# A planned one-core attention kernel: a new table of shifts for its planner, and one more pack of scores for VectorE

## The chip, the cores and the metric

The kernel runs on one core of a Trainium2 chip. The metric is the time of one execution on the device in microseconds. Five engines work side by side: TensorE (PE, with its weight loads as PEld), ScalarE (ACT), VectorE (DVE), GpSimd (POOL), and SyncE (SP), which here only issues DMAs.

## The reference

Two attention blocks read the same input x (2048 tokens of 512, bf16), and a gate mixes their outputs. Block A is softmax attention with 32 heads of 16; block B is linear attention whose features are softmaxes of a learned projection of q and k.

```python
def _A_ref(x, wqkv, wo):
    # q, k, v: 32 heads of 16
    scores = jnp.einsum("bhqd,bhkd->bhqk", q, k) * (Dh ** -0.5)
    p = _softmax(scores, axis=-1)
    o = jnp.einsum("bhqk,bhkd->bhqd", p, v)
    return (lambda x, *d: x.transpose(*d))(o, 0, 2, 1, 3).reshape(B, S, D) @ wo

def _B_ref(x, wqkv, w_phi, wo):
    pq = jnp.einsum("bhsd,hdf->bhsf", q, w_phi)
    pk = jnp.einsum("bhsd,hdf->bhsf", k, w_phi)
    phi_q = jnp.concatenate([_softmax(pq, axis=-1), _softmax(-pq, axis=-1)], axis=-1)
    phi_k = jnp.concatenate([_softmax(pk, axis=-1), _softmax(-pk, axis=-1)], axis=-1)
    kv = jnp.einsum("bhsf,bhsd->bhfd", phi_k, v)
    z  = jnp.einsum("bhsf->bhf", phi_k)
    num = jnp.einsum("bhqf,bhfd->bhqd", phi_q, kv)
    den = jnp.einsum("bhqf,bhf->bhq", phi_q, z)[..., None] + 1e-6
    o = num / den
    return (lambda x, *d: x.transpose(*d))(o, 0, 2, 1, 3).reshape(B, S, D) @ wo

x = A_x
g = _sigmoid((x * gate_w).sum(-1, keepdims=True))
return g * a + (1 - g) * b
```

## The kernel before

**Units and packs.** Block A's scores are cut into units: 128 keys by 512 queries of one head. Four units, four heads of one key tile, make a pack, and there are 512 packs (4 query chunks, 8 groups of heads, 16 key tiles), so 2048 units. A group of scores is written by TensorE (`_scores`, L1013: the contraction over 16 features, zero-padded to 32 rows, takes one of four row strips of the array, so that up to four units share one pass) into a ring of five PSUM banks. ScalarE's exp (L1061, called "exp k" below) reads three units and two units in turn, 1536 or 1024 elements a partition, and writes them to `ET`. The scores of exp k wait for exp k-2, which frees their banks. TensorE then multiplies the exps of a pack with the values (`_values`, L1128, four matmuls of 32 columns, one in each column strip) and adds them up in one PSUM bank for the 16 key tiles of a group.

**Packs for VectorE.** For some packs the exponential isn't made by ScalarE. `AWAY` holds, for each of the 32 groups, five bits: which of the key tiles 1, 4, 7, 10 and 13 go to VectorE. There, `_vector_bits` (L932) turns each unit's scores with one multiply and add into the bits of a bf16 number, which is a rough power of two (`va`), and `_vector_terms` adds two shifted copies of it (`vp`): one by VectorE (L954, for two packs at once 4096 elements wide, for one alone 2048), and one by GpSimd (L969, in two halves a pack). TensorE sums the three terms through the value matmuls (L1128, with `V`, or with `vc`, the scaled values). The units that are left over for ScalarE are grouped three and two in their own order.

**The rest of the work** fills the engines around this: projections of q, k and v (L654 and L727, four matmuls a bank, with a VectorE copy out of PSUM), the product of block B's weights with its feature projection (L1226 transposes them, L1244 multiplies; both need the weights `WB` from DRAM), block B's softmaxes in quads of token tiles (VectorE's tree of maxima L1290, the subtraction L1299, ScalarE's exp L1301 over 2048 elements, twice a quad, then sums and a reciprocal), its sums kv (L1347) and quotients (L1405, L1411, L1413), and the outputs (`_b_out` L1431 and `_out` L1477, copied out by L1490, at the end by L1472, L1483 and L1487). A group's attention is normalized by VectorE (L1149 transposes it out of PSUM, then L1156, L1158, L1160) and turned by DMAs on SP's queue, of the last two groups by VectorE again (L1165). Nine matmuls on a constant tile warm TensorE up at the start (L641).

**The planner.** Nothing of the order is written by hand. Each instruction is an `Op` with an engine, a cost that the author has set, its dependencies, a priority and an earliest pack, and `Plan.order` places them one by one: of the instructions that are ready it takes the one with the lowest priority number. The resulting order of each engine is fixed at build time, and each engine runs its queue strictly in that order, waiting on semaphores. Two lists steer it:

```python
def order(self):
    for o in self.ops:

        d = self.shift.get(o.tag, 0)
        o.prio += d
        o.rel += d if o.rel > -90 else 0
```

`SHIFT` names tags (`b103` is the bits of pack 103, `p10` the value matmuls of pack 10, `k`, `q`, `v` projections, `e`, `h` and others block B's parts, `g` a group's normalization, `y` the outputs) and a number that moves the tag's instructions to earlier or later, in packs.

**Use of the array.** The planner keeps a running sum of how much of the array the matmuls of the last 3 us used, with a score or a value matmul counting a quarter. Where it is low, it adds idle matmuls whose result is zero or is overwritten: `_fill` (L1135, four at a time, in an open accumulation) and whole matmuls ahead of a group of scores (L1034).

```python
low = lambda share: sum(r[1] for r in recent) < share * self.SPAN
while o.filler > o.filled and low(self.SHARE) or (
        o.pad and self.open is None and o.filled < self.PADS and low(self.PAD)):
    o.filled += 1
    recent.append((t, self.FILL))
```

Of the kernel before, what the change touches and what calls it, by code (L numbers as in the profile page):

```python
# [388 lines left out]
class _Kernel:  # L389
# [348 lines left out]
    def _gate(self):  # L738
# [44 lines left out]
    AWAY = (19, 27, 21, 30, 11, 27, 28, 30, 31, 31, 15, 15, 21, 23, 31, 27, 27, 31, 29, 29, 29, 31, 13, 15, 31, 15, 28, 21, 15, 31, 22, 31)  # L783

    SHIFT = (
# [103 lines left out]
    def _plan_vector(self):  # L889
# [3 lines left out]
        pairs = []  # L893
        for g, bits in enumerate(self.AWAY):
            packs = [self.NT * g + self.KT0 + self.KTS * n for n in range(self.NKT) if bits >> n & 1]
# [642 lines left out]
```

## Time and profile before

| | before |
|---|---|
| median of 3 runs | 750.57 us (744.85, 750.57, 750.6) |
| profiled execution, its own time | 745.28 us |
| its span, first to last instruction | 743.5 us |
| ACT busy | 728.4 us (98%) |
| PE busy | 707.1 us (95%) |
| DVE busy | 692.0 us (93%) |
| POOL busy | 277.3 us (37%) |
| mean granted TensorE clock | 0.999 |

The busy time of an engine is the union of its instructions' times. The mean duration of a group can be longer than the pace at which its instructions follow each other, since an engine starts the next before the last has left it; where a number depends on that, the pace is taken from a stretch without idle time. A row of groups reads: line, engine, operation, tiles, shapes and count; then busy time and mean ns of one; then the idle time just before them and what ended it. A row of the chain or the timeline reads: start and length in us, then what ran, and in brackets the idle time before it.

### The profile page before, as it was taken

To read this page: it belongs to the slowest core of one execution; us is meant where nothing else is said; L and a number is where in the kernel's file an instruction comes from. 1 tells how busy PE (TensorE), PEld (TensorE's weight loads), DVE (VectorE), ACT (ScalarE), POOL (GpSimd) and SP (SyncE) were. 2 spreads that over 40 slices of the span, in tenths; PEclk is the share of its full clock that TensorE was granted. 3 is DMA by queue.
4 is the path that set the end of the run, shared out by engine and by line. 5 is a ranking of instruction groups with operands and counts; after the bars stand their busy time and mean duration, and the time that the engine had idled before them with its cause. 6 is when DMAs were issued, how large, how long until landed. Compare 5 with 4: busy or idle time off the path is not lost.

```text
span 743.5 us, 17213 instructions
## 1 busy us (share of the span) xinstructions
PE 707.1 (95%) x7255; PEld 226.9 (31%) x7320; DVE 692.0 (93%) x1093; ACT 728.4 (98%) x636; POOL 277.3 (37%) x275
## 2 busy tenths in 40 slices
PE   8999999999899999999998999999999999999997
PEld 4334234342232222322322233222232223322332
DVE  6898989999998999999999999989999989999994
ACT  5999999999999999999999999999999999999996
POOL 6521331513335534233252442244432253235431
PEclk9999999999999999999999999999999999999999
DMA  9300100101000000000000411220111032104110
GB/s 203 138 9 4 20 4 10 15 2 15 8 12 12 5 17 5 12 11 8 8 10 11 69 16 30 56 48 13 16 37 30 19 67 23 30 20 82 23 23 29
DMA packets 90030, 21.80 MB, mean 29 GB/s; under 512 B 82912, under 2 KB 89440, under 8 KB 89952
## 3 DMA queue, kind: packets, MB, share of 16 engines
q1 hardware_dynamic: 88224, 20.17, 14.1%
q8 instruction: 57, 0.93, 0.6%
q10 hardware_dynamic: 1728, 0.52, 0.3%
q14 instruction: 21, 0.17, 0.1%
HBM read 4.21 MB, written 2.10 MB: 8 GB/s over the span
## 4 chain that ended last, share of the span: by engine, by line
ACT 89%; PE 7%; SPq 2%; DMA 1%; DVE 1%; issue 0%
ACT ET L1061 85%; ACT bq L1301 4%; PE ps L1013 2%; PE ps L1128 2%; PE ps L654 1%; SPq L1383 1%; DMA WB<-in_B_wqkv_dram 1%; PE ps L1431 0%; PE ps L1477 0%; SPq L527 0%; PE ps L727 0%; SPq L542 0%; DVE va L932 0%; ACT xT L1487 0%; DVE VB L1259 0%
## 5 line engine op out<-in xcount | busy, mean ns | idle before, releaser
L1061 ACT ACTIVATE ET<-ps 128x1536 bf16<-128x1536 f32 x616 | 700.9, 1363 | 6.2 <-PE ps L1013 6.0
L969 POOL TENSOR_SCALAR vp<-va 128x1024 uint16<-128x1024 uint16 x258 | 269.5, 1044 | 454.5 <-DVE va L932 120.7
L932 DVE TENSOR_SCALAR va<-ps 128x512 uint16<-128x512 f32 x508 | 332.2, 682 | 22.4 <-PE ps L1013 19.6
L1013 PE MATMUL ps<-qT,kT 32*128 32x512 bf16 x2048 | 310.2, 384 | 15.2 <-ACT ET L1061 8.4
L1013 PEld LDWEIGHTS ps<-qT,kT 32*128 32x128 bf16 x2048 | 81.3, 91 | 265.7 <-ACT ET L1061 160.2
L954 DVE TENSOR_SCALAR vp<-va 128x4096 uint16<-128x4096 uint16 (+1 forms) x143 | 157.7, 1109 | 1.2 <-PE ps L1128 0.8
L1128 PE MATMUL ps<-ET,V 128*32 128x512 bf16 x1540 | 146.1, 385 | 0.2 <-DVE va L932 0.2
L1128 PE MATMUL ps<-vp,vc 128*32 128x512 bf16 x1016 | 91.0, 384 | 1.4 <-DVE vp L954 1.4
L1135 PE MATMUL ps<-kT,zero 128*32 128x512 bf16 x628 | 56.1, 385 | 0.0
L1128 PEld LDWEIGHTS ps<-ET,V 128*32 128x32 bf16 x1540 | 38.0, 95 | 58.7 <-issue 46.8
L654 PE MATMUL ps<-WB,xT 128*128 128x512 bf16 x166 | 50.0, 383 | 4.9 <-issue 2.7
L1128 PE MATMUL ps<-va,V 128*32 128x512 bf16 x508 | 49.8, 385 | 0.0
L1128 PE MATMUL ps<-vp,V 128*32 128x512 bf16 x508 | 46.8, 384 | 1.5 <-DVE vp L954 1.2
L1128 PEld LDWEIGHTS ps<-vp,vc 128*32 128x32 bf16 x1016 | 23.8, 95 | 35.8 <-issue 21.8
L654 PE MATMUL ps<-xT,WA 128*128 128x512 bf16 (+1 forms) x104 | 30.3, 373 | 4.3 <-issue 3.1
L1301 ACT ACTIVATE bq<-bq 128x2048 bf16<-128x2048 bf16 x16 | 32.5, 2035 | 0.0
L1149 DVE STREAM_TRANSPOSE T<-ps 128x512 f32<-128x512 f32 x32 | 22.7, 708 | 5.9 <-PE ps L1128 5.8
L1272 DVE CAST bq<-ps 128x512 bf16<-128x512 f32 x32 | 21.9, 685 | 3.4 <-PE ps L654 3.1
L1135 PEld LDWEIGHTS ps<-kT,zero 128*32 128x32 bf16 x628 | 14.2, 94 | 23.2 <-issue 20.8
L727 PE MATMUL ps<-WA,xT 128*128 128x128 bf16 x256 | 20.5, 220 | 0.2 <-DVE WB L1249 0.2
L1299 DVE TENSOR_TENSOR bq<-bq,btree 128x2048 bf16<-128x2048 bf16 x16 | 20.0, 1248 | 0.1
L654 PEld LDWEIGHTS ps<-WB,xT 128*128 128x128 bf16 x192 | 12.0, 97 | 24.2 <-issue 13.5
(84 smaller groups left out, 343.3 us busy)
## 6 DMA issues: line engine op xcount, KB each, us to landing
turned<-T SPq DMA_DIRECT2D x240, 8.0 KB, 1.8
qT<-qs SPq DMA_DIRECT2D x120, 16.0 KB, 1.8
WB<-in_B_wqkv_dram SPq DMA_DIRECT2D x1, 1536.0 KB, 7.8
out_dram<-WB SPq DMA_DIRECT2D x12, 128.0 KB, 1.7
WA<-in_A_wqkv_dram SPq DMA_DIRECT2D x3, 384.0 KB, 4.6
WoA<-in_A_wo_dram SPq DMA_DIRECT2D x1, 512.0 KB, 8.8
WoB<-in_B_wo_dram SPq DMA_DIRECT2D x1, 512.0 KB, 9.5
WA<-in_A_wqkv_dram ACTq DMA_DIRECT2D x3, 128.0 KB, 4.3
```

Of the source, the lines that this page charges most:

```text
L654: ins = e.matmul(self._bank(job)[:, 0:n], lhs(c), rhs(c), start=(c == 0), stop=(c == 3))
L727: ins = e.matmul(self._bank(job)[:, P * tt:P * tt + P], self.xT[:, c, QCH * j + TOK * tt:QCH * j + TOK * tt + TOK], self.WA[:, 2, c, P * c ...
L932: parts.append(op("DVE", lambda e, j=j, job=job: e.tensor_scalar(self.va[:, pair, side, j, :], self._bank(job), SCALE * LOG2E * 128.0, (12 ...
L954: self.plan.op("DVE", lambda e, k=k, shift=shift: e.tensor_scalar(flat(self.vp[:, k]), flat(self.va[:, pair]), float(shift), None, op0=ALU ...
L969: o = self.plan.op("POOL", lambda e, flat=flat: e.tensor_scalar(flat[0], flat[1], 1.0, float(shift), op0=ALU.mult, op1=ALU.add), 0.08 + n ...
L1013: return e.matmul(out, self.kT[32 * i:32 * i + 32, cp, kt * TOK:(kt + 1) * TOK], self.qT[32 * i:32 * i + 32, s, :], start=True, stop=True, ...
L1061: o = plan.op("ACT", lambda e: e.activation(self.ET[:, a % NS:a % NS + n, :], self.ps[:, self._ring(a):self._ring(a) + n, :], ACT.Exp, sca ...
L1128: ins = e.matmul(self._bank(ot)[32 * i:32 * i + 32, :], V[:, v0:v0 + 32], tile(), start=(kt == 0), stop=(kt == self.NT - 1), tile_position ...
L1135: ins = e.matmul(self._bank(ot)[32 * i:32 * i + 32, :], self.zero[:], self.kT[:, 0, 0:QCH], start=False, stop=False, tile_position=(0, 32 ...
L1149: op("DVE", lambda e: e.transpose(T1[:, side].rearrange("p b s -> p (b s)"), src()), 0.635, deps=last, writes=[b_T1[side]], name="n_t1", p ...
L1272: [lambda e, b, k=k: e.tensor_copy(bq[:, k].rearrange("p (g s v) -> p g s v", g=8, s=2)[:, :, 0, :], b.rearrange("p (g v) -> p g v", g=8))],
L1301: op("ACT", lambda e, side=side: e.activation(sides[side], sides[side], ACT.Exp, scale=1.0 - 2 * side), self.c_act(2048) + 0.04, reads=[bu ...
```

## The change

Only the two tables differ. `AWAY` has 128 bits set instead of 127 and places them otherwise; `SHIFT` has 759 entries instead of 753, nearly all of them new. No function, constant or cost is changed. The author's words for it: the order of work was searched anew, with a charge (in the search, which isn't part of the kernel) for stretches in which TensorE's array is little used; 128 packs for VectorE.

```diff
-    AWAY = (19, 27, 21, 30, 11, 27, 28, 30, 31, 31, 15, 15, 21, 23, 31, 27, 27, 31, 29, 29, 29, 31, 13, 15, 31, 15, 28, 21, 15, 31, 22, 31)
+    AWAY = (23, 26, 30, 22, 27, 26, 21, 27, 31, 15, 31, 30, 19, 15, 22, 30, 31, 31, 15, 31, 28, 31, 30, 30, 30, 31, 21, 15, 29, 15, 30, 31)
 
     SHIFT = (
-        ("a0", -0.5), ("b1", -5.5), ("b103", -11), ("b106", -3.5), ("b109", -11.5), ("b116", -0.5), ("b122", -13),
...
-        ("x81", -2.5), ("x84", 11.5), ("x90", 7.5), ("x93", -14), ("y128", -10.5), ("y256", -0.5), ("y512", -14)
+        ("a0", 1.5), ("a12", -3.5), ("a4", 0.5), ("a8", -6), ("b1", -1), ("b103", 1), ("b113", -4), ("b116", 2.5),
...
+        ("y128", 8), ("y512", -3)
     )
```

Since every engine's order follows from these numbers, nearly every instruction stands elsewhere. Counted in the two built programs, the kinds and numbers of instructions differ in this alone:

| engine, line | before | after |
|---|---|---|
| ACT L1061, 1536 / 1024 / 512 elements | 308 / 308 / 0 | 307 / 307 / 1 |
| DVE L932 | 508 | 512 |
| DVE L954, 4096 / 2048 elements | 109 / 34 | 111 / 32 |
| POOL L969 | 258 | 260 |
| PE L1128, from ET / from va and vp | 1540 / 2032 | 1536 / 2048 |
| PE L1135, fills | 628 | 604 |
| PE L1034, whole matmuls ahead of scores | 15 | 24 |

198 rows, old and new, of the table SHIFT are left out of this document.

## The prediction

> **What bounds the kernel now.** I read the page's first part and its chain, then what ACT waits for, then ACT's groups by form, then the few places where ACT idles, in time.
>
> ```profile
> PE 707.1 (95%) x7255; PEld 226.9 (31%) x7320; DVE 692.0 (93%) x1093; ACT 728.4 (98%) x636; POOL 277.3 (37%) x275
> ACT 89%; PE 7%; SPq 2%; DMA 1%; DVE 1%; issue 0%
> ACT ET L1061 <- PE ps L1013: 6.0, 3, 5.4
> ACT xT L1487 <- PE ps L1477: 3.6, 1, 3.6
> ACT L1061 <- issue: 2.3, 1, 2.3
> ACT ET L1061 <- PE ps L1128: 0.2, 1, 0.2
> ```
>
> PE, DVE and ACT all look full, but only ACT is full by necessity. Its waits (the last four lines: total, times, longest) are 5.4 us for the first scores, 3.6 us at the very end, 2.3 us before the table load, and about 0.8 us in the middle. In between the exps of L1061 run end to end for some 726 us; any work of PE, DVE, POOL or SP that lands in time costs nothing. So the time is: start to first exp, plus ACT's own work, plus ACT's idle time, plus the tail. The question for each edit is which of the four it touches.
>
> ```profile
> L1061 ACT ACTIVATE ET<-ps 128x1536 bf16<-128x1536 f32 x308 | 484.3, 1573 | 6.2 <-PE ps L1013 6.0 <-PE ps L1128 0.2
> L1061 ACT ACTIVATE ET<-ps 128x1024 bf16<-128x1024 f32 x308 | 355.2, 1153 | 0.0
> L1301 ACT ACTIVATE bq<-bq 128x2048 bf16<-128x2048 bf16 x16 | 32.5, 2035 | 0.0
> 120.51 67.85 ACT ET L1061 x60
> 273.48 1.79 ACT bq L1301
> ```
>
> The mean durations overlap (484.3 + 355.2 is more than the 700.9 us of the page's group), so I price exps by the chain's stretch: 60 in 67.85 us are 30 pairs of 2.262 us, five score units a pair. The forms differ by 1573 - 1153 = 420 ns for 512 elements, so a 1536 costs 1.34 us of the row, a 1024 0.92 us, and a 512 (no row) about 0.92 - 0.42 = 0.50 us.
>
> **The change, part by part.** *128 packs instead of 127.* Counted in the two orders, ACT has 308 + 308 exps before and 307 + 307 plus one of 512 after: 2.262 - 0.50 = **1.76 us less**. Bounds: 2.26 if the short exp were free, 2.262 - 0.92 = 1.34 if it cost as much as a 1024. I take 1.76, by the difference of the forms.
>
> ```profile
> L932 DVE TENSOR_SCALAR va<-ps 128x512 uint16<-128x512 f32 x508 | 332.2, 682 | 22.4 <-PE ps L1013 19.6
> L954 DVE TENSOR_SCALAR vp<-va 128x4096 uint16<-128x4096 uint16 x109 | 134.1, 1236 | 0.5 <-PE ps L1128 0.2
> L954 DVE TENSOR_SCALAR vp<-va 128x2048 uint16<-128x2048 uint16 x34 | 23.7, 700 | 0.6 <-PE ps L1128 0.6
> L969 POOL TENSOR_SCALAR vp<-va 128x1024 uint16<-128x1024 uint16 x258 | 269.5, 1044 | 454.5 <-DVE va L932 120.7
> L1135 PE MATMUL ps<-kT,zero 128*32 128x512 bf16 x628 | 56.1, 385 | 0.0
> L1034 PE MATMUL ps<-kT 128*128 128x512 bf16 x9 | 3.4, 383 | 0.4 <-issue 0.3
> ```
>
> The pack goes to DVE: 4 more L932 (4 x 0.682 = 2.7 us), two more wide L954 and two fewer narrow ones (2 x 1.236 - 2 x 0.700 = 1.1 us), 3.8 us in all; POOL gets 2 more L969 (2.1 us). PE gets 4 fewer matmuls of ET, 16 more of va and vp (net +12, four to a pass); the fills of L1135 go from 628 to 604 and the pads of L1034 from 15 (the row holds the records of 9) to 24. A pass or a full matmul paces at 0.22 us (below), so +0.7 - 1.3 + 2.0 = +1.4 us. None is on ACT's path: DVE ends at about 696 of 742 us, PE at 708, POOL at 279. Without that cover DVE's 3.8 us would be the whole price.
>
> *The new order at the start.* Before, PE meets L1226 after its 14th group of scores, and L1226 needs the weights WB.
>
> ```profile
> 16.48 7.75 DMA WB<-in_B_wqkv_dram
> 24.28 0.62 PE L1226 MATMUL ps<-iden,WB 128*128 128x128 bf16 x8 [0.45 <-DMA WB<-in_B_wqkv_dram]
> 25.27 3.84 ACT L1061 ACTIVATE ET<-ps 128x1536 bf16<-128x1536 f32 x3 [0.34 <-PE ps L1013]
> 102.83 2.37 ACT L1061 ACTIVATE ET<-ps 128x1536 bf16<-128x1536 f32 x2 [0.15 <-PE ps L1128]
> 105.53 1.45 ACT L1061 ACTIVATE ET<-ps 128x1536 bf16<-128x1536 f32 x1 [0.33 <-PE ps L1013]
> 70.40 0.54 PE ps L654 x2
> 96.51 0.97 PE ps L654 x4
> ```
>
> WB lands at 24.23; PE stood still 0.45 us, the scores behind L1226 came late, ACT idled 0.34 us. After, the first L1226 stands behind 28 groups, some 14 pairs x 2.262 = 32 us after the first exp: WB has then been there for 16 us. **0.34 us back.** SP's queue up to WB, WoA and WoB is the same, so nothing of the loads is later. The other loads that PE meets early keep slack: x512, landed by 9.9 us, is met after 2 groups instead of 3, at about 10.2 us.
>
> At 102 to 106 us PE itself was short: 4.00 us busy of 4.00, and ACT idled 0.15 + 0.33. Between the 50th and the 100th exp the order has 56 matmuls of L654 and 96 of L727 before, 52 and 80 after. L654 paces at (0.97 - 0.54) / 2 = 0.215 us, a 128-wide L727 at a quarter: 4 x 0.215 + 16 x 0.054 = 1.7 us less for PE there. **0.48 us back** (0 at the least, if the shortage moves).
>
> *The new order at the pairs of L1301.* Scores for exp k wait for exp k-2, so in an L1301 PE runs dry unless other work stands there. The new order puts two L1301 back to back or one exp apart at the 82nd, 473rd and 549th exp, with 4.1, 3.3 and 4.5 us of array work beside them. The tightest is the 549th.
>
> ```profile
> L1490 DVE CAST WB<-ps 128x512 bf16<-128x512 f32 x12 | 8.2, 685 | 0.0
> L1290 DVE TENSOR_TENSOR btree<-btree 128x128 bf16<-128x128 bf16 x16 | 3.5, 218 | 0.0
> L1156 DVE TENSOR_TENSOR rinv<-T,gh 128x32 f32<-128x32 f32 x15 | 2.9, 193 | 0.0
> L1299 DVE TENSOR_TENSOR bq<-bq,btree 128x2048 bf16<-128x2048 bf16 x16 | 20.0, 1248 | 0.1
> ```
>
> From the start of the exp before the first L1301, ACT wants the second after 1.34 + 1.79 + 0.92 = 4.05 us. DVE must by then have done L1490, L1290, L1156, L932 and L1299: 0.685 + 0.218 + 0.193 + 0.682 + 1.248 = 3.0 us, and L1490 waits for an output matmul about 1.0 us in. That is 4.0 us: on the edge, where every L1301 before started without a wait. Bounds 0 and 0.6 us (one DVE copy out of place); I take **0.1 us**, since the durations overlap by some 10%.
>
> *The tail.*
>
> ```profile
> 735.92 0.40 PE L1128 MATMUL ps<-ET,V 128*32 128x512 bf16 x4
> 736.38 0.72 DVE L1149 STREAM_TRANSPOSE T<-ps 128x512 f32<-128x512 f32 x1 [4.41 <-PE ps L1128]
> 25.22 0.55 PE ps L1128 x8
> 26.09 0.33 PE ps L1128 x4
> ```
>
> Before, the last L1149 follows the last four matmuls of ET. After, four of vp stand behind those and L1149 waits for them too: 0.55 - 0.33 = **0.22 us more**. What follows is the same chain. The SP queue is reordered (transfers of qs, T, phiT, nb, out), but counted along both orders the waits on them by PE and DVE keep 0.9 us or more.
>
> Sum on the profiled execution: 745.28 - 1.76 - 0.34 - 0.48 + 0.1 + 0.22 = **743.0**. The page's execution is 0.4 us above the lowest of the runs shown, 744.85, from which the same terms give 742.6. I forecast **742.8**. With the bounds: 744.85 - 2.26 - 0.82 = 741.8 and 745.28 - 1.34 - 0.34 + 0.6 + 0.22 = 744.4.
>
> **Where the 750 comes from.** Of four executions, two took 744.85 and 745.28, two 750.57 and 750.6. The trace shows only the quick kind. A place where it could tip:
>
> ```profile
> 180.00:200.00 20.00, 17.69 (x189) 5.45 (x188) 19.42 (x29) 20.00 (x18) 5.51 (x6) 1.00 0.03 7
> 188.00:192.00 4.00, 3.04 (x46) 0.96 (x38) 3.97 (x5) 4.00 (x4) 0.00 (x0) 1.00 0.11 27
> 192.00:196.00 4.00, 2.81 (x39) 0.95 (x39) 3.90 (x7) 4.00 (x5) 0.78 (x1) 1.00 0.03 6
> 740.00:743.50 3.50, 0.00 (x0) 0.00 (x0) 0.57 (x1) 0.58 (x2) 0.00 (x0) 0.84 0.45 150
> L641 PE MATMUL ps<-bq 128*128 128x512 bf16 x9 | 3.9, 619 | 1.5 <-DVE bq L574 1.5
> ```
>
> In these windows PE's busy time is the first number after the width and the clock the third from the end. PE is thinnest at 188 to 196 us and the clock stayed 1.00; with PE empty, after 740, it falls. The only slow matmuls of the trace, the nine warm-ups at its start, take 3.9 / 9 = 0.43 us each instead of 0.215; I take that as the price of the lower clock. Counting how much of the array each matmul of the two orders uses (a score or a 32-wide value matmul a quarter), with scores placed where ACT's pace lets them start, the leanest 3.4 us use about 0.30 of the array before (near 190 us; next 0.34 near 397) and 0.41 after. So if the two long executions had a lower clock, the new order should not have it.
>
> [...]
>
> **Rivals.** *Two kinds of executions remain* (0.18): the 5.3 to 5.7 us come from something the order doesn't touch, such as the start (the nine warm-up matmuls are unchanged) or the chip. Then the median can fall on the long kind: 750.57 - 2.3 = 748.3. For it: the two long ones agree within 0.03 us. Against: nothing in the trace.
>
> *The pack is saved and eaten* (0.08): the change doesn't do what it says; the DVE edge at the 549th exp, the shortage at 102 us moved elsewhere and later transfers take 2 us. 745.3. For it: DVE's 93%. Against: the counted margins.
>
> *Slower: the array starves at the pairs of L1301* (0.12). [...]
>
> **How the numbers follow.** The forecast has 0.62, with a range of its own of 741.6 to 744.4. A measurement of this kernel can tell about 1% from no change; 1% below the median of 750.57 is 743.06, just above my forecast, so its chance splits: 0.42 below, 0.20 above; of the second rival 0.01 falls below. Faster 0.43; same 0.20 + 0.18 + 0.07 + 0.03 = 0.48; slower 0.09, the rest of the last rival. The range goes from the lower bound to above the first rival: 741.5 to 749.5, leaving out the slower rival and some at the low end.
>
> **What would show it.** ACT x635, with about 726.7 us busy; no idle before L1061 at 25 us and at 102 to 106 us; L1226 not waiting for WB; the last L1149 0.2 us later after the last exp; clock 1.00 to the end; L1301 waiting at most 0.6 us near 659 us. A clock below 1 in the middle, or ACT idle over 1.5 us between first and last exp, would prove me wrong; executions near 748 would show that the order isn't what parts the two kinds.

## The result, and the profile after

| | before | after |
|---|---|---|
| median | 747.36 us (8 runs, 744.85 to 750.6) | 742.62 us (8 runs, 742.27 to 743.4) |
| ratio after to before, 95% interval | | 0.9934 (0.9908 to 0.9961) |
| profiled execution, its own time | 745.28 us | 742.71 us |
| its span | 743.5 us | 740.9 us |
| ACT busy / PE busy | 728.4 / 707.1 us | 726.5 / 709.5 us |

The forecast was 742.8. The 4.7 us between the medians are two things. Of the eight executions of before four are short (744.85, 745.21, 745.52, 745.58) and four long (749.13, 749.77, 750.57, 750.6), and the median lies between the kinds; of after none is long. The median of the short ones, 745.4, is 2.7 us above after's; the other 2.0 us are the long kind, which none of after's eight shows.

The page of after, the parts that answer to those shown of before (engines, the chain, then WB's load with its KB and its us from issue to landing):

```profile
PE 709.5 (96%) x7261; PEld 226.2 (31%) x7317; DVE 694.9 (94%) x1097; ACT 726.5 (98%) x635; POOL 279.7 (38%) x277
ACT 87%; PE 11%; DMA 1%; DVE 1%; issue 0%; DVEq 0%
WB<-in_B_wqkv_dram SPq DMA_DIRECT2D x1, 1536.0 KB, 7.0
```

ACT's waits (total, times, longest), then its groups by form, of after:

```profile
ACT ET L1061 <- PE ps L1013: 5.1, 2, 4.9
ACT xT L1487 <- PE ps L1477: 3.8, 1, 3.8
ACT L1061 <- issue: 2.3, 1, 2.3
...
L1061 ACT ACTIVATE ET<-ps 128x1536 bf16<-128x1536 f32 x307 | 491.5, 1601 | 5.3 <-PE ps L1013 5.1
L1061 ACT ACTIVATE ET<-ps 128x1024 bf16<-128x1024 f32 x307 | 362.7, 1181 | 0.0
L1061 ACT ACTIVATE ET<-ps 128x512 bf16<-128x512 f32 x1 | 0.8, 767 | 0.0
```

ACT bounds the kernel as before. Its visible waits in the middle went from 0.8 us to about 0.4. The mean durations rose (1573 to 1601 ns, 1153 to 1181) although the work per exp is the same: an exp enters before the previous one has left (by 0.24 us in before and 0.27 in after, in the median), and a mean counts that overlap too. Where exps run back to back, the next starts 1331 ns (1536 elements) or 904 ns (1024) later, in both traces, and 1800 ns after an L1301. The one exp of 512 elements is the last, so its pace isn't seen; by the step of 427 ns it would be 477.

The stretches that the prediction named, in after: windows (width, then busy PE, PEld, DVE, ACT, POOL, then clock, DMA share, GB/s), then the timeline.

```profile
24.00:25.40 1.40, 1.40 (x19) 0.33 (x15) 1.40 (x2) 1.40 (x2) 0.21 (x1) 1.00 1.09 356
100.00:106.00 6.00, 6.00 (x43) 2.50 (x42) 5.36 (x9) 6.00 (x5) 0.00 (x0) 1.00 0.01 3
188.00:192.00 4.00, 4.00 (x54) 1.22 (x53) 4.00 (x9) 4.00 (x5) 2.09 (x2) 1.00 0.01 4
192.00:196.00 4.00, 4.00 (x49) 1.14 (x45) 3.97 (x10) 4.00 (x5) 2.75 (x3) 1.00 0.00 0
...
8.51 2.37 ACT L1061 ACTIVATE ET<-ps 128x1536 bf16<-128x1536 f32 x2 [4.91 <-PE ps L1013]
11.06 2.37 ACT L1061 ACTIVATE ET<-ps 128x1536 bf16<-128x1536 f32 x2 [0.18 <-PE ps L1013]
39.73 0.39 PE L1226 MATMUL ps<-iden,WB 128*128 128x128 bf16 x4
656.74 1.22 DVE L1299 TENSOR_TENSOR bq<-bq,btree 128x2048 bf16<-128x2048 bf16 x1
657.99 2.01 ACT L1301 ACTIVATE bq<-bq 128x2048 bf16<-128x2048 bf16 x1
...
733.80 0.72 DVE L1149 STREAM_TRANSPOSE T<-ps 128x512 f32<-128x512 f32 x1 [2.10 <-PE ps L1128]
736.92 1.09 ACT L1487 ACTIVATE xT<-ps 128x512 bf16<-128x512 f32 x2 [3.84 <-PE ps L1477]
```

ACT has no idle time at 25 us nor at 102 to 106. The first L1226 stands at 39.73 us and waits for nothing (WB was issued at 16.9 and landed at 23.9). PE is full at 188 to 196 us. The L1301 near 658 starts 0.03 us after its L1299 ends (656.74 + 1.22 = 657.96). It shows no idle time before it, but it starts 1.02 us after the 1024 ahead of it, where that pace is 0.904: it waited 0.12 us for L1299, hidden in the overlap of the two.

Starts of all exps compared, the 2.58 us between the spans (743.45 and 740.87) are:

| part of the span | before | after | change |
|---|---|---|---|
| start to the first exp | 8.96 | 8.51 | -0.45 |
| exps and L1301 at the paces above, first start to last | 716.28 | 714.94 | -1.33 |
| the last exp itself (1024, now 512 elements) | 1.20 | 0.77 | -0.43 |
| what starts come later than those paces | 9.44 | 8.86 | -0.58 |
| end of the last exp to the end | 7.58 | 7.79 | +0.21 |

Of the fourth row only 0.84 and 0.42 us show as idle time in the middle; the rest are late starts, nearly all by less than 0.24 us, which hide in the overlap.

### The profile page after: what moved, and what is told of

Read it like the earlier page. It is cut to its first block, busy times and chain, and to the rows that moved or that the text cites. A ratio compares the mean times of both kernels' runs of the same rounds, so it can differ in the third digit from the quotient of the medians.

```text
span 740.9 us, 17208 instructions
## 1 busy us (share of the span) xinstructions
PE 709.5 (96%) x7261; PEld 226.2 (31%) x7317; DVE 694.9 (94%) x1097; ACT 726.5 (98%) x635; POOL 279.7 (38%) x277
## 4 chain that ended last, share of the span: by engine, by line
ACT 87%; PE 11%; DMA 1%; DVE 1%; issue 0%; DVEq 0%
ACT ET L1061 83%; PE ps L1128 4%; PE ps L1013 4%; ACT bq L1301 4%; PE ps L654 1%; DMA xT<-in_A_x_dram 1%; PE ps L1431 1%; PE ps L1477 0%; PE ps L1405 0%; PE ps L1135 0%; PE ps L727 0%; DVE va L932 0%; DVE qT L710 0%; ACT xT L1487 0%; PE ps L1034 0%
## 5 line engine op out<-in xcount | busy, mean ns | idle before, releaser
L1061 ACT ACTIVATE ET<-ps 128x1536 bf16<-128x1536 f32 x615 | 698.9, 1390 | 5.3 <-PE ps L1013 5.1
L969 POOL TENSOR_SCALAR vp<-va 128x1024 uint16<-128x1024 uint16 x260 | 271.9, 1046 | 448.5 <-DVE vp L954 151.6
L932 DVE TENSOR_SCALAR va<-ps 128x512 uint16<-128x512 f32 x512 | 336.4, 684 | 19.9 <-PE ps L1013 16.7
L1013 PE MATMUL ps<-qT,kT 32*128 32x512 bf16 x2048 | 310.4, 384 | 13.6 <-ACT ET L1061 6.5
L1013 PEld LDWEIGHTS ps<-qT,kT 32*128 32x128 bf16 x2048 | 80.5, 91 | 262.4 <-ACT ET L1061 159.6
L954 DVE TENSOR_SCALAR vp<-va 128x4096 uint16<-128x4096 uint16 (+1 forms) x143 | 158.6, 1115 | 0.6 <-PE ps L1128 0.3
L1128 PE MATMUL ps<-ET,V 128*32 128x512 bf16 x1536 | 144.7, 385 | 0.9 <-issue 0.3
L1128 PE MATMUL ps<-vp,vc 128*32 128x512 bf16 x1024 | 93.3, 385 | 0.8 <-POOL vp L969 0.4
L1128 PEld LDWEIGHTS ps<-ET,V 128*32 128x32 bf16 x1536 | 38.0, 95 | 61.1 <-issue 46.5
L1135 PE MATMUL ps<-kT,zero 128*32 128x512 bf16 x604 | 52.6, 384 | 0.0
L1128 PE MATMUL ps<-va,V 128*32 128x512 bf16 x512 | 50.5, 385 | 0.0
L1128 PE MATMUL ps<-vp,V 128*32 128x512 bf16 x512 | 47.1, 384 | 0.6 <-DVE vp L954 0.4
L1128 PEld LDWEIGHTS ps<-vp,vc 128*32 128x32 bf16 x1024 | 24.4, 95 | 39.5 <-issue 25.3
L654 PE MATMUL ps<-xT,WA 128*128 128x512 bf16 (+1 forms) x109 | 32.0, 374 | 3.5 <-issue 1.9
L1301 ACT ACTIVATE bq<-bq 128x2048 bf16<-128x2048 bf16 x16 | 32.3, 2056 | 0.0
L1128 PEld LDWEIGHTS ps<-va,V 128*32 128x32 bf16 x512 | 13.4, 95 | 20.5 <-issue 16.1
L1299 DVE TENSOR_TENSOR bq<-bq,btree 128x2048 bf16<-128x2048 bf16 x16 | 19.5, 1218 | 0.0
```

The lines of the kernel that those rows point to most:

```text
L654: ins = e.matmul(self._bank(job)[:, 0:n], lhs(c), rhs(c), start=(c == 0), stop=(c == 3))
L932: parts.append(op("DVE", lambda e, j=j, job=job: e.tensor_scalar(self.va[:, pair, side, j, :], self._bank(job), SCALE * LOG2E * 128.0, (12 ...
L954: self.plan.op("DVE", lambda e, k=k, shift=shift: e.tensor_scalar(flat(self.vp[:, k]), flat(self.va[:, pair]), float(shift), None, op0=ALU ...
L969: o = self.plan.op("POOL", lambda e, flat=flat: e.tensor_scalar(flat[0], flat[1], 1.0, float(shift), op0=ALU.mult, op1=ALU.add), 0.08 + n ...
L1013: return e.matmul(out, self.kT[32 * i:32 * i + 32, cp, kt * TOK:(kt + 1) * TOK], self.qT[32 * i:32 * i + 32, s, :], start=True, stop=True, ...
L1061: o = plan.op("ACT", lambda e: e.activation(self.ET[:, a % NS:a % NS + n, :], self.ps[:, self._ring(a):self._ring(a) + n, :], ACT.Exp, sca ...
```

## The experiments

All kernels are before or after with one edit to the planned queues or to single instructions in them (e8 has two); the rest of the order stays. "Before beside" is the kernel before on the same chip; the ratios, with their intervals, are not the quotients of the medians. Inserted lines move the line numbers by 2 to 14 (L1061 becomes L1065 in most, L1013 L1017, L1226 L1230). Theories: the long kind comes from *lean stretches* of the array in the middle (the prediction's), or from a *wait at the start* for WB, or from something the order doesn't touch.

| run | edit | us (runs) | ratio to before beside, 95% |
|---|---|---|---|
| e1 | before, lean stretches padded | 751.66 (5) | 1.0085 (1.0073 to 1.0097) |
| e2 | before, WB issued 4 us earlier | 745.58 (11) | 1.0007 (0.9998 to 1.0015) |
| e3 | after, no idle matmuls | 769.73 (6) | 1.0328 (1.0302 to 1.0353) |
| e4 | before, WB behind WoA and WoB | 750.12 (4) | 1.0076 (1.0061 to 1.0091) |
| e5 | after, WB behind WoA and WoB | 742.32 (6) | 0.9968 (0.9956 to 0.9979) |
| e6 | before again | 744.66 (10) | 0.9993 (0.9984 to 1.0003) |
| e7 | after, four exps one unit shorter | 741.28 (4) | 0.9956 (0.9941 to 0.9971) |
| e8 | e4, 13 matmuls ahead of L1226 | 748.35 (10) | 1.0032 (1.0013 to 1.0051) |
| e9 | before, WB ahead of three parts of WA | 744.95 (10) | 0.9992 (0.9974 to 1.0010) |
| e10 | before again | 745.11 (10) | 0.9988 (0.9970 to 1.0006) |
| e11 | before, L1226 doesn't read WB | 744.61 (12) | 0.9988 (0.9976 to 1.0001) |
| e12 | after again | 742.25 (6) | 0.9953 (0.9934 to 0.9971) |

**e1: are lean stretches the cause?** One whole idle matmul is added ahead of each group of scores in the leanest stretches of before, 31 in all.

```diff
+for k in [*range(155, 167), *range(241, 246), *range(329, 336), *range(521, 528)]:
+    self.qks[k].filled += 1
```

> The order of before, with one more whole matmul (L1034) ahead of 31 groups of scores: exps 155-166, 241-245, 329-335 and 521-527, where the array was used least (near 190-206, 291-298, 399-407 and 624-632 us). Theory clock: the executions near 750 are those in which the clock fell in one of these stretches; then all executions are near 745.3 (744.8 to 746.3, since a pad costs 0.22 to 0.32 us and PE has some 0.4 us before each group), all at clock 1.00. Rival WB: nothing changes, two kinds remain, 745.3 and 750. Rival outside the order: the same as rival WB.

Measured: 751.66 beside 744.91, every clock 1.00. ACT's first wait of e1:

```profile
ACT ET L1063 <- PE ps L1015: 9.5, 13, 5.0
```

Thirteen waits where before has three. The waits that show are 3.5 us more than before's; the rest are late starts hidden in the overlap, since all starts together came 7.5 us later than in before's profile, of it 0.4 at L1226, where WB came later for PE. 31 pads at 0.22 us are 6.8 us, and the kernel became 6.75 us longer: nearly every pad lay on the path. A group of scores may start only when the exp two before has freed its bank, and the pad stands between that and the scores; the exp then comes later by the pad. PE was thinly used there but not free. A miss for both theories, and no test of the long kind either: of the 17 executions of before beside it none was over 746.

**e2: does an earlier issue of WB end the wait at 25 us?** WB's DMA moves ahead of wphi's on SP's queue.

```diff
+sp.remove(wb)
+sp.insert([o.name for o in sp].index("dma_wphi"), wb)
```

> The order of before, with the DMA of WB issued ahead of those of w_phi and gate_w on SP's queue, 2.6 us earlier. Theory clock: two kinds remain; the quick kind is 0.3 us shorter (745.0), since PE no longer waits at L1226, the long kind near 750 stays with a clock below 1. Rival WB: the long kind is one in which WB lands 5 us late; with 2.6 us of head start it shrinks to 747 or below, the quick kind is 745.0. Rival outside the order: two kinds, 745.0 and 750, clock 1.00 in both.

The chain and ACT's timeline of e2:

```profile
12.64 11.68 DMA WB<-in_B_wqkv_dram
25.35 4.75 ACT L1065 ACTIVATE ET<-ps 128x1536 bf16<-128x1536 f32 x4 [0.71 <-PE ps L1017]
30.76 4.63 ACT L1065 ACTIVATE ET<-ps 128x1536 bf16<-128x1536 f32 x4 [0.65 <-PE ps L1017]
```

WB was issued at 12.64 instead of 16.48 us and landed at 24.32 instead of 24.23. What it was moved past is only some 17 KB, so nearly the same bytes stood ahead of it, and the landing stayed where it was, though the issue came 3.8 us sooner (e9 below moves it past 1.15 MB more). wphi, which it was moved past, landed at 24.52 instead of 18.98 us, and a second wait came. Nothing gained.

**e3: what is the price of a lean array?** All idle matmuls (L1135 and L1034) of after are left out; they add nothing to the result.

```diff
+p.queues["PE"] = [o for o in p.queues["PE"] if o.name != "pad"]
+for o in p.queues["PE"]:
+    o.filled = 0
```

> The order of after without its idle matmuls (all fills L1135 and pads L1034 taken out; they add nothing to the result). Theory clock: the array's use falls by 175 passes, the leanest 3.4 us by about a third, the clock falls in the middle in every execution, and the time is 748 to 780 us. Rivals WB and outside the order: PE has 38 us less to do and is not the bound, so 742.3 to 743.4 as after, or 0.3 us less, with clock 1.00.

Measured 769.73, mean clock 0.929 to 0.941. Clock, ACT's first wait and four windows of e3:

```profile
core 0: 767.5 us, clock 0.940
ACT ET L1064 <- PE ps L1016: 27.4, 30, 5.0
200.00:207.00 7.00, 4.69 (x49) 1.41 (x47) 7.00 (x14) 7.00 (x6) 1.05 (x1) 1.00 0.07 16
207.00:214.20 7.20, 6.57 (x56) 1.19 (x48) 5.74 (x8) 6.25 (x6) 2.47 (x3) 0.53 0.13 16
272.00:279.10 7.10, 7.10 (x55) 1.65 (x47) 4.63 (x9) 5.40 (x5) 2.09 (x2) 0.52 0.00 0
716.00:733.20 17.20, 16.46 (x109) 3.63 (x109) 12.85 (x22) 13.44 (x13) 6.28 (x6) 0.50 0.16 24
```

The clock (third from the end) is 1.00 in the first of these windows, with PE busy 4.69 of 7.00 us, and 0.53, 0.52 and 0.50 in the others. ACT waits 30 times for scores, 27.4 us in all, and the time is 27 us longer than after's 742.62. So here the idle matmuls kept the clock up (after's mean is 1.000), as the prediction supposed of a fuller array; whether before was lean enough to lose it is another matter.

**e4, e5, e6: the wait at L1226.** WB's DMA moves behind those of WoA and WoB, in before (e4) and in after (e5); e6 is before unchanged.

```diff
+sp.remove(wb)
+sp.insert([o.name for o in sp].index("dma_wob") + 1, wb)
```

> The order of before, with WB's DMA issued behind those of WoA and WoB on SP's queue (in the profile the last of the three lands 2.9 us after WB). Theory WB (PE waits at L1226 for the landing, and the wait goes to ACT one for one): ACT idles 0.3 + 2.9 = 3.2 us at L1226, and the time is 2.9 us longer than before, 747.8. Rival: PE catches up later, under 1 us longer.

> The order of after with the same later WB. Theory WB: L1226 stands some 16 us later, so nothing changes: 742.3 to 743.4, no idle time at L1226. Rival: as long as e4 against its own base, 745.5.

> Before unchanged, once more, for its profile and the clock of each run. If an execution near 750 falls to it: theory WB expects WB landing some 5 us later than 24.2 us and ACT idle at L1226 for it; theory clock expects a clock below 1 in several windows; theory outside the order expects idle or longer ACT time spread over the span.

The chain, timeline and windows of e4:

```profile
18.01 8.57 DMA WB<-in_B_wqkv_dram
26.63 0.70 PE L1230 MATMUL ps<-iden,WB 128*128 128x128 bf16 x8 [2.79 <-DMA WB<-in_B_wqkv_dram]
27.93 2.56 ACT L1065 ACTIVATE ET<-ps 128x1536 bf16<-128x1536 f32 x2 [2.98 <-PE ps L1017]
32.04 2.54 ACT L1065 ACTIVATE ET<-ps 128x1536 bf16<-128x1536 f32 x2 [1.55 <-PE ps L1017]
34.86 1.45 ACT L1065 ACTIVATE ET<-ps 128x1536 bf16<-128x1536 f32 x1 [0.29 <-PE ps L1017]
...
23.50:27.00 3.50, 0.71 (x14) 0.54 (x11) 0.82 (x2) 1.45 (x2) 1.05 (x1) 1.00 0.56 225
27.00:30.40 3.40, 3.40 (x24) 0.64 (x21) 1.84 (x3) 2.39 (x2) 0.29 (x1) 0.50 0.02 5
30.40:33.80 3.40, 3.40 (x28) 0.63 (x31) 2.20 (x4) 1.79 (x3) 1.05 (x1) 0.50 0.00 0
33.80:37.20 3.40, 3.40 (x51) 1.00 (x43) 2.49 (x5) 3.11 (x4) 2.06 (x2) 0.99 0.00 0
```

WB landed at 26.58 us, 2.35 later than in before's profile, in which the first exp starts at the same time (8.96 and 8.98). PE stood 2.79 us at L1226 (L1230 here), ACT idled 2.98, then the clock was 0.50 in the next two windows, 6.8 us in all, and ACT idled 1.55 + 0.29 us more. The time, 750.12 beside 745.06, is 2.3 us more than the theory's 747.8, and it is that of the long executions. In e5 WB landed at 26.0 too (17.0 + 9.0), ACT had no wait there, and the time is after's own, 742.32: the new order doesn't feel a late WB.

e6, before unchanged, gave 744.66 and no long execution among ten; in its profile WB landed at 23.45.

**e7: are 1.76 us for the exps the right term?** In after, the exps 100, 220, 340 and 460 take two units instead of three; four units of the output then use old exps.

```diff
+for k in (100, 220, 340, 460):
+    at = 5 * (k // 2)
+    self.exps[k].fn = lambda e, at=at: e.activation(
+        self.ET[:, at % 30:at % 30 + 2, :], self.ps[:, self._ring(at):self._ring(at) + 2, :], ACT.Exp, scale=SCALE)
```

> After, with one unit less in each of four exps (1536 elements become 1024 in exps 100, 220, 340 and 460, so four units of the output use old exps): the price of the pack that the change took from ACT. Theory ACT-bound: 4 x 0.42 = 1.7 us less, 740.9. Rival (PE at 96% and DVE at 94% are about to bind): under 0.8 us less, 741.9 or more.

Measured 741.28: 1.04 less than e5 on the same chip, 1.34 less than after's first runs, where four units at 427 ns (1331 - 904) are 1.7. ACT's timeline of e7 around exp 340 (L432 is the shortened one):

```profile
410.77 1.26 ACT L432 ACTIVATE ET<-ps 128x1024 bf16<-128x1024 f32 x1
411.77 4.83 ACT L1065 ACTIVATE ET<-ps 128x1024 bf16<-128x1024 f32 x4
```

It is 1.00 us to the next start, not 0.904, and from that start to the one after it 1.12 us: the scores aren't there sooner, probably since PE's order was timed for the longer exp. No idle time shows here; behind two of the other three shortened exps 0.10 and 0.12 us do. Both theories missed: with the old order a unit less was worth only a part of its pace. In the change itself, planned anew, it was worth all of it: the late starts of the table above did not grow.

**e8, e9, e10: the stall and the clock apart.** e8 is e4 with 13 whole matmuls ahead of the first L1226, so that PE works while it would stand. e9 issues WB ahead of three parts of WA (the last two lines of the cut below). e10 is before again.

```diff
+def fill(e):
+    for _ in range(13):
+        ins = e.matmul(self._bank(first.acquire), self.kT[:, 0, 0:P], self.kT[:, 0, 0:QCH], start=True, stop=True)
+    return ins
...
+pe.insert(pe.index(first), x)
...
+sp.remove(wb)
+sp.insert([o.name for o in sp].index("dma_wa11"), wb)
```

> e4 (before, WB behind WoA and WoB) with 13 whole matmuls on a free bank in front of the first L1226, 2.8 us that PE would otherwise stand still. Theory: of e4's 5.1 us only the late landing itself stays, ACT idle some 3 us at L1226, and the clock stays 1.00, so the 2.0 us that ACT lost after it go: 747.5 to 748.2. Rival: the second part isn't the clock's but comes from PE's queue catching up; then 750 as e4.

> Before, with WB's DMA ahead of the three later parts of WA, so that WB lands some 4 to 5 us earlier (near 20 us) and PE doesn't wait at L1226. Theory WB: no idle time of ACT near 25 us, 744.2 to 744.6 on a chip where before takes 745.0, and no execution above 746 anywhere. Rival: the loads behind it come late instead and cost as much, 745 or more.

> Before unchanged on whichever chip this falls, for an execution near 750 and its clock. Theory WB with clock: such an execution has a clock of 0.993 to 0.996 (two windows at half), as e4 had, and in its profile WB lands after 26 us. Theory outside the order: a clock of 0.999 to 1.00.

Windows and timeline of e8:

```profile
23.50:27.00 3.50, 3.03 (x18) 1.24 (x16) 0.69 (x1) 1.26 (x2) 1.04 (x1) 1.00 0.52 205
27.00:30.40 3.40, 3.40 (x43) 1.23 (x47) 2.77 (x5) 2.46 (x3) 0.29 (x1) 1.00 0.02 5
27.92 4.75 ACT L1075 ACTIVATE ET<-ps 128x1536 bf16<-128x1536 f32 x4 [3.16 <-PE ps L1027]
```

WB landed at 26.89 (17.43 + 9.46) and ACT idled 3.16 us at L1226, as in e4, but the clock stayed 1.00 and no second wait came. The time is a little over the theory's 748.2. 748.35 - 745.09 (before beside) = 3.3 us against 750.12 - 745.06 = 5.1 in e4: of a late WB 3.3 us are the wait and 1.8 went with the 6.8 us at clock 0.50.

Beside these three, 25 executions of before: 19 from 744.21 to 746.27, and six of 747.35 to 749.89, at mean clocks 0.999, 0.997, 0.997, 0.995, 0.995 and 0.995. The 6.8 us at 0.50 take 3.4 of the 748.4 us of e4's profiled execution off its mean, which is 0.995: the three longest have the mean clock that it has.

In e9 WB landed at 18.3 us and the wait at 25 us is gone, but wphi landed at 23.2 and something else came late:

```profile
29.48 5.97 ACT L1065 ACTIVATE ET<-ps 128x1536 bf16<-128x1536 f32 x5 [0.61 <-PE ps L1017]
```

Nothing gained (744.95): taking this wait away by the loads' order puts another in its place. Two of its ten executions, 746.07 and 747.14 (clock 0.998), lie above the 746 that the theory allowed; neither was profiled, and what made them longer is not shown. e10 gave 745.11 and no long execution.

**e11, e12: before without the wait.** In e11 L1226 (`wtr`) transposes x in place of WB, so PE needn't wait for WB at this point, and block B's projected weights are those of other data; WB is waited for only where block B's weights are written to SBUF, some time later. e12 is after again.

```diff
+if o.name == "wtr":
...
+            ins = e.transpose(bank[:, 512 * c2 + P * cp:512 * c2 + P * cp + P],
+                              self.xT[:, c, P * cp:P * cp + P], self.iden[:])
...
+    o.deps = [d for d in o.deps if d is not wb]
+if o.name == "wphi_ev":
+    o.deps.append(wb)
```

> Before, with the transposes of L1226 reading x instead of WB (so block B's projected weights are those of other data), at the same place of the same order, and WB's landing waited for only by the copy L1249, some 12 us later. Theory WB with clock: the executions of before at 747 to 750 come from the wait at L1226, so here all are at 744.0 to 746.0 with a clock of 0.997 or more, and the median is 0.2 to 0.5 us under before's. Rival (the two half-speed windows lie elsewhere, in a lean stretch such as 188 to 196 us): as many executions over 747 as before has beside it.

> After unchanged, beside before on the same chip. Theory WB with clock: 742.0 to 743.4 in every execution, clock 0.997 to 1.00, while before has some at 747 to 750 with 0.993 to 0.996. Rival (the long kind belongs to the chip): after has long executions too.

Measured 744.61, twelve executions from 744.23 to 745.1; beside them before had 749.27 (clock 0.995) and 747.46 (0.997) among 17. Twelve are few beside 2 of 17, so the count alone proves little. But in e11's own profile WB happened to land late. Its load (issue, then us to landing) and ACT's timeline are:

```profile
L557 SPq DMA_DIRECT2D WB<-in_B_wqkv_dram x1: 434/434/434, 17.4 to 17.4; - x1
DMA to landing us min/median/max: 8.7/8.7/8.7
...
9.38 30.87 ACT L1074 ACTIVATE ET<-ps 128x1536 bf16<-128x1536 f32 x27 [5.78 <-PE ps L1026]
```

Landed at 26.1 us with nothing moved on SP's queue, 1.9 us later than in before's profile, while the first exp was 0.42 later; ACT ran through 25 us without a gap and that execution took 745.1. In the profiles of before, e1, e2, e4 and e10 PE comes to L1226 14.9 us after the first exp; by that it would here have stood for some 1.85 us. e12 gave 742.25, no execution above 743.39.

Over all runs: of after 14 executions, and 6 more with the late WB of e5, none above 743.4. Of before, unchanged and timed beside these: 4 of 8, 0 of 17, 1 of 15, 6 of 25, 2 of 17 above 747, and none of 20 in e6 and e10. That is 13 of 102, so 14 without a long one are no proof by themselves. None of the long executions of before was itself profiled. That its WB landed late is inferred from e4 (the same time and clock when it is made late), e11 (none where the wait is absent, and a landing at 26.1 by itself) and after (no wait at L1226 in any profile); it wasn't seen. For the first four long ones, of up to 750.6, no clock is on record either, and nothing shows why their share differs so between the chips.

## Why the prediction was right, and where it was not

**Exps, -1.76.** Right to the hundredth: -1.33 up to the last start and -0.43 in the last exp. The by-form difference of mean durations (420 ns for 512 elements) was close to that of the paces (427). That both prices were too high made no difference: a pair paces at 2.235 us, not 2.262, which held some late starts, and the short exp comes to 0.477 by the same step, not 0.50.

**L1226, -0.34: right place, wrong size.** This is the term that was mis-sized, and the 2.0 us of the long kind hung on it, as far as the runs show. The wait was priced from one execution, in which WB landed 0.45 us late for PE. Over the nine profiles with nothing moved on SP's queue ahead of WB its landing lay between 23.3 us (e7) and 26.1 us (e11), eight of them by 24.3. In e4 the landing came 2.35 us later and ACT's wait grew by 2.64, and another 1.8 us (e4 against e8) went with the clock. The price of this place was nothing in e6 and 5.1 us more than before's in e4; between these it depends on the execution.

**"Where the 750 comes from": the right kind of cause, by the runs the wrong place.** That the long kind would go came out, but not for the reason given, which is luck: the new order was expected to part from it by its fuller stretches, and what took it away, by the runs, is the later L1226. A lower clock was part of it, as said, but the place, as inferred above, was the stand at 25 us, not the lean stretches near 190 and 397 us, where before's clock is 1.00 in its profile (188 to 196 and 396 to 400 us). Some executions have a lower mean clock without the long time: at 0.997 two executions on e1's chip took 745.64 and 745.71, beside 744.91, and two of e11, which can't wait at L1226, took 744.97 and 745.02 beside 744.61; where in them the clock was lower is not shown. Counted in the prediction's way, but from the matmuls in before's trace, the leanest 3.4 us use 0.36 of the array near 190 us, not 0.30, and 0.35 near 398, and after's leanest (near 130 us) 0.36, not 0.41; some matmuls are missing from both traces. That the clock hangs on this share was the author's estimate, and no run shows from which share on it would fall. The prediction looked for lean stretches of the planned order and didn't ask what a longer wait would do to the one wait that it had already found.

**102 to 106 us, -0.48.** The idle time there is gone as said; new small waits (0.18 us at 11.06, 0.07 at 29, 0.05 at 463, 0.11 at 717) took back 0.42 of the 0.84 that was lost before. With those that don't show, the starts' lateness fell by 0.58 in all, against 0.34 + 0.48 - 0.1 = 0.72 forecast.

**The pair at 658 us, +0.1.** Right: the L1301 starts 0.12 us late, right behind its L1299, on the edge as worked out. What was wrong is that every L1301 before started without a wait: by the paces the one at 190.12 us started 0.20 late, hidden in the overlap. **Tail, +0.22.** It was +0.21.

**Not foreseen: the first exp 0.45 us earlier.** The first load of x landed at 5.54 instead of 5.98 us. Over all profiles, whose instructions up to there are the same but for one score matmul, the first exp lay between 8.38 and 9.38 us with before's order and between 8.47 and 8.71 with after's, so most of this is the execution's. Without it, the profiled difference would be 2.13 us; the forecast's terms make 2.26, and the 0.14 of late starts is what lacks. That the result came so near 742.8 owes something to this start, which is luck.

**The rivals.** *Two kinds remain*: not borne out, none of after's executions is long. *Saved and eaten*: wrong, the DVE edge cost its 0.1 us and the pack's saving came whole. *Slower, the array starves at the L1301 pairs*: wrong, after's mean clock is 1.000. That an order with the idle matmuls left out loses clock and time, at other places, e3 shows: a mean of 0.940 over 767.5 us, which would be some 92 us at 0.50 (an estimate from these numbers), and a span 26.6 us longer than after's.

## What to carry to other kernels

A wait for a DMA that sits on the path is to be priced by the spread of that landing over executions, not by the one in the trace: here 0.34 us in the profile, and 5.1 more when the load landed 2.35 us later; the remedy was to put the reader of the load 15 us later, not to issue the load earlier. An engine with idle time between its pieces isn't free at the point where its work is timed to the critical engine: 31 idle matmuls cost their full 6.8 us. And a saving on the critical engine is whole only if the engines that feed it are planned anew for it: 1.0 to 1.3 of 1.7 us with the old order.

## What the runs showed of the hardware

The granted clock in four places: in e4 PE was busy 0.71 of 3.50 us (it stood 2.79 us at L1226); in the 6.8 us after that the clock was 0.50, though PE was busy throughout, and in the next 3.4 us 0.99. In e8, with 13 matmuls in the place of the stand, PE was busy 3.03 of 3.50 us and the clock stayed 1.00. In e3, without the idle matmuls, it was 0.53 from 207.0 to 214.2 us, behind 7.00 us in which PE was busy 4.69 (0.67 of the time); in before PE was busy 2.81 of 4.00 us (0.70) at 192 to 196 us, and the clock stayed 1.00. What parts the last two places, the busy time of PE, the share of the array or another thing, is not shown, nor how little work is too little.

The landing of the 1.5 MB of WB behind other loads went with the bytes ahead of it: issued at 12.64 (e2) or 16.48 us (before) with nearly the same bytes ahead, it landed at 24.32 and 24.23; issued at 10.79 us ahead of three parts of WA (1.15 MB, e9) it landed at 18.3. With the order of before it also landed at 26.1 us once (e11), and why is not shown. And in the traces of before and after an ACT instruction starts 0.24 and 0.27 us in the median (0.1 to 0.4) before the one ahead has left, so a wait as short as the 0.12 us at 658 us leaves no idle time; only the distance from start to start shows it.
